# Reordering ScalarE's and VectorE's work in the first groups of a fused retention and feed-forward kernel

## The chip, the cores and the metric

The kernel runs on one core of a Trainium2 chip. The metric is the device time of one execution in microseconds, as the median of several runs. Five engines work beside one another, each on a queue of its own: TensorE (PE, with its weight loads shown apart as PEld), VectorE (DVE), ScalarE (ACT), GpSimd (POOL) and SyncE (SP), which here issues nearly all transfers.

## The reference

Two stages follow one another, in float32 (the weights arrive as 64-bit numbers and are converted on the chip).

```python
# retention: 4 batches, 8 heads, 768 steps, head size 64
for t in range(S):
    state = gamma * state + k[t] (outer) v[t]
    y[t]  = scale * (q[t] @ state)
# x is y with its heads side by side: 3072 tokens by 512
h   = x @ w_in                       # 512 -> 2048
sp  = max(h, 0) + log1p(exp(-|h|))   # softplus
g   = h * erf(sp)
out = g @ w_out                      # 2048 -> 512
```

## The kernel before

**Retention.** The 768 steps of a batch are cut into chunks of 128 tokens, 24 chunks in all. A chunk `j` passes through six steps, written as one-letter names from line 872 on: `K_` scales keys and queries (VectorE, line 403, later 393 and 400), `T` transposes them (TensorE line 418 with ScalarE copies at 424; from chunk 6 on VectorE does it alone, line 413), `S_` forms the scores (TensorE, line 431 or 508), `M` masks them (VectorE, line 443 or 515), `O_` forms the output and the state's increment (TensorE, lines 471, 478 and 487, copied out by ScalarE at 498), and `A` adds the increment to the state (VectorE, line 611).

**Feed-forward, first tile.** The first 512 tokens go through plain products. `hidden(g, u)` forms hidden product `ft = 4 g + u`: four matmuls of 128 x 512, eight records in the trace (line 664), then a copy by ScalarE (line 682). The four products of a group `g` fill one buffer `h`; `gate(g)` runs softplus (line 624) and erf (line 634) over it, each behind a load of its function table; `gated(g)` multiplies h by the result (line 653); `project(g, tt)` multiplies by w_out (line 700). Hidden products use two PSUM banks in turn (`ps_h`), so product `ft` can start only when product `ft - 2` has been copied out. Retention's scores, transposes and outputs share two other banks (`ps_r`).

**Feed-forward, the rest.** From group `G0 = 4` on, 256 tokens at a time go through seven products in place of eight (`hidden_part`, line 757, and `project_part`, line 829). VectorE forms the sums that this needs: of weights at line 248, of x at 740, of the products at 770, 777 and 782.

**Weights.** Each weight piece is loaded raw into parts of the weight buffers that are not in use yet. A conversion takes five VectorE instructions (lines 213, 217, 222, 225, 231) and one ScalarE instruction (line 214), which reads what line 213 wrote and is read by line 225. When line 225 is done the raw piece isn't needed any more, and the next load into its place may be issued. The first four pieces are converted in halves, one product's weights each. `need(...)` drives conversions until the named tile is there; `pace(n)` drives some steps of it between other work. So weight conversion and retention share VectorE's queue, and what is written first in the program stands first in it.

**The order around the change.** A table `after` holds, for each of the first four groups and each of its four products, two lists of calls: those made at once behind the product, and those put on the list `waiting`, which the next paced place empties half-way through its share of weight steps. The loop `for g in range(G0)` reads the table. Behind projection steps of group 3 stand chunk 6's `K_` and `T` and, at the last one, chunk 7's. The loop `for g in range(G0, NG)` does the seven-product groups; `first` marks group 4.

Of the kernel before, what the change touches and what calls it, by code (L numbers as in the profile page):

```python
# [22 lines left out]
FG = 4  # L23
# [22 lines left out]
def kernel(  # L46
# [21 lines left out]
    JPC = TCH // C  # L68
# [67 lines left out]
    def w_out_of(ft):  # L136
        half, s, i = ft // (2 * FG), ft % (2 * FG) // FG, ft % FG
        return w_out_sb[:, s, 2 * half : 2 * half + 2, i, :]
# [115 lines left out]
    def weights():  # L254


        pending = [conversion(n) for n in range(n_p)]
        begun = 0
        for n, steps in enumerate(pending):
            for k, _ in enumerate(steps, start=begun):  # L260
                yield
                if n > 4 and n + 1 < n_p and k == 2:
                    next(pending[n + 1])
                    yield
            begun = int(n > 4)
            if pieces[n] == ("out", 5):
                yield from sums("in", 0)
# [5 lines left out]
    weight_steps = weights()  # L273
# [11 lines left out]
    def need(*what):  # L285
        nonlocal room
        while what not in done:
            if next(weight_steps, done) is done:
                next(last_steps)
            room -= 1  # L290
# [315 lines left out]
    def ret_add(j):  # L606
        if j not in SU:
            return
        new = SU[j]
        if j % NC:  # L610
            nc.vector.tensor_tensor(state, state, new, op=ALU.add)
        else:
            nc.vector.tensor_copy(state, new)
        pace(-0.4)
# [4 lines left out]
    def gate(g):  # L619


        name = "r" if g < 4 and g % 2 else "e"
        E[g] = act.tile([P, N], F32, name=name, bufs=1)
        nc.scalar.activation(E[g], HS[g], AF.Softplus)  # L624

        if g:
            gate_erf(g)
# [10 lines left out]
    def pace_around(n):  # L638


        pace(n / 2)
        run(waiting)
        waiting.clear()
        pace(n / 2)

    def run(steps):
        for f, *args in steps:
            f(*args)

    def gated(g):  # L650
        for a in range(2):
            half = slice(a * N // 2, (a + 1) * N // 2)
            nc.vector.tensor_tensor(E[g][:, half], HS[g][:, half], E[g][:, half], op=ALU.mult)  # L653
        pace(-2.2)
# [4 lines left out]
    def hidden_of(ft, t):  # L659

        if ft not in HP_:
            HP_[ft] = ps_h.tile([P, TCH], F32, name="hp")
        for kk in range(n_k):
            nc.tensor.matmul(  # L664
                HP_[ft][:, t], w_in_of(ft, kk), XC[0][:, kk, t],
                start=(kk == 0), stop=(kk == n_k - 1),
            )

    def hidden(g, u):
        ft = g * FG + u  # L670
        if u == 0:
            HS[g] = act.tile([P, N], F32, name="h")
        need("in", ft)
        if ft == 0:
            hidden_of(1, slice(TCH - C))
        hidden_of(ft, slice(TCH) if ft > 1 else slice(TCH - C, TCH))

        if ft < FG:
            need("in", ft + 2)
        if ft == 0:  # L680
            ret_add(JPC - 1)
        nc.scalar.copy(HS[g][:, u * TCH : (u + 1) * TCH], HP_.pop(ft))  # L682
        done.add(("hidden", ft))
        if ft == FG - 1:
            need("in", FG + 3)
        if g:
            pace_around(3.4 if ft > FG else 0)

    def project(g, tt):
        if g == 0 and tt == 0:  # L690
            O[0] = [ps_o.tile([P, d_model], F32, name=f"o{i}") for i in range(TT)]
        step = tt
        if g:
            of = [(tt, u) for u in range(FG)]
        else:
            of = [(step % 2 * 2 + i // 2, step // 2 * 2 + i % 2) for i in range(4)]
        need("out", g * FG + max(u for _, u in of))
        for tt, u in of:
            ft = g * FG + u
            nc.tensor.matmul(  # L700
                O[0][tt].rearrange("p (d c) -> p d c", d=2),
                E[g][:, u * TCH + tt * P : u * TCH + (tt + 1) * P],
                w_out_of(ft),
                start=(ft == 0),
                stop=(ft == n_ft - 1),
            )
        if step == TT - 1:
            done.add(("project", g))
        pace_around(3.4)
# [10 lines left out]
    G0 = n_ft // FG  # L720
# [5 lines left out]
    def chunk_of(g):  # L726
        return TCH // SCH + (g - G0) // 2
# [74 lines left out]
    def g_sums(g):  # L802

        e = {name: E[g][:, i * TCH : (i + 1) * TCH] for name, i in HQ.items()}

        x = {"11": e["11"], "12": e["21"], "21": e["12"], "22": e["22"]}
        for i in range(4):
            x[f"S{i + 1}"] = HS[g][:, i * TCH : (i + 1) * TCH]
        for to, a, b, plus in (
            ("S1", "21", "22", 1), ("S2", "S1", "11", 0), ("S3", "11", "21", 0), ("S4", "12", "S2", 0),  # L810
        ):
            nc.vector.tensor_tensor(x[to], x[a], x[b], op=ALU.add if plus else ALU.subtract)
        G[g] = x
        pace(-2.4)
# [29 lines left out]
    def put_part(m, step):  # L844
# [27 lines left out]
    K_, T, S_, M, O_, A = (  # L872
        ret_scale, ret_transpose, ret_scores, ret_mask, ret_out, ret_add
    )
# [6 lines left out]
    for j in range(JPC - 2):  # L881
# [3 lines left out]
        if j:  # L885
# [27 lines left out]
    after = [  # L913
        [([], [])] * FG,
        [
            ([(K_, 4), (next, weight_steps), (gate_erf, 0), (load, 5)], []),
            ([], []),
            ([(T, 4)], []),
            ([(S_, 4)], []),
        ],  # L920
        [
            ([(O_, 4)], [(A, 4)]),
            ([(T, 5)], []),
            ([(S_, 5)], [(M, 5)]),
            ([(O_, 5), (load_block_scales,)], [(A, 5)]),
        ],
        [
# [7 lines left out]
    for g in range(G0):  # L935
        for u in range(FG):

            if g and u == (2 if g == 1 else 0):
                waiting.append((gated, g - 1))
            hidden(g, u)  # L940
            run(after[g][u][0])
            if (g, u) == (1, 0):
                room = 0.0
            waiting.extend(after[g][u][1])
        gate(g)
        if g:
            for tt in range(TT):
                project(g - 1, tt)
                if g == 1 and tt < 2:
                    waiting.append((K_, 5) if tt else (M, 4))  # L950
                elif g == G0 - 1 and tt == 0:
                    waiting.extend([(K_, JPC + 2), (T, JPC + 2)])
                elif g == G0 - 1 and tt == 1:
                    load(JPC + 4)
                elif g == G0 - 1 and tt == 3:
                    K_(JPC + 3)
                    T(JPC + 3)

    j = JPC + 2
    put = None
    for g in range(G0, NG):
        first = g == G0
        more = j < NJ
        hidden_part(g, 1)
        hidden_part(g, 2)
        if first:
            gated(g - 1)
        if put is not None:  # L970
            for step in range(3):
                put_part(put, step)
        hidden_part(g, 6)
        if first:
            S_(j)
            M(j)
        for _ in range(2):
            next(last_steps, None)
        if put is not None:
            put_part(put, 3)  # L980
            put = None
        if not first:
            g_sums(g - 1)
        hidden_part(g, 5)
        hidden_part(g, 7)
        for _ in range(2):
            next(last_steps, None)
        if first:
            project(g - 1, 0)
        else:  # L990
            project_part(g - 1, 1)
        hidden_part(g, 4)
        hidden_part(g, 3)


        if more and not first:
            sub_visit(j, g)
        elif more:
            O_(j)
            A(j)  # L1000
            SC[j + 1] = [ret_psum(ps_h) for _ in range(2)]
            sub_scores(j + 1)
            sub_mask(j + 1)
        if g + 1 < NG and (g - G0) % 2:
            x_sums(g + 1)
        if more:
            if j + 2 < NJ:
                K_(j + 2)
                T(j + 2)
            if j + 3 < NJ:  # L1010
                load(j + 3)
            j += 1
        if first:
            gate(g)
            for tt in range(1, TT):
                project(g - 1, tt)
            put_first()
        else:
            for p in (2, 4):
                project_part(g - 1, p)  # L1020
            gate(g)
            for p in (5, 6, 7, 3):
                project_part(g - 1, p)
            if (g - G0) % 2 == 0:
                put = chunk_of(g - 1)
        if g == NG - 1:
            last_gated(g)
        else:
            gated(g)

    g, m = NG - 1, chunk_of(NG - 1)
# [55 lines left out]
```

## Time and profile before

| | before |
|---|---|
| time, median of 3 (lowest, highest) | 686.38 us (686.1, 686.8) |
| span of the profiled run | 684.8 us |
| granted TensorE clock | 1.00 |
| VectorE busy, 40.00 to 50.00 | 9.79 of 10.00 us |
| VectorE busy, 60.00 to 70.00 | 9.86 of 10.00 us |
| VectorE busy, 121.18 to 134.90 | 7.12 of 13.72 us |
| one hidden product of 512 tokens on TensorE | 3.43 us (13.74 for four) |
| softplus or erf over a group, with its table load | 1.28 + 1.91 us |
| one VectorE conversion of a whole piece | about 5 us in five instructions |

The first 165 us hold the plain groups, retention's first chunks and all weight conversions; from there on a period of two groups repeats every 26.8 us to the end. The profile lists, for each instruction, its start, its duration and, in square brackets, how long its engine sat idle before it and what ended that. A matmul's end is modelled, so a distance between starts tells more than a busy time.

### The profile page before, as it was taken

What the parts mean: (1) busy time and instruction counts of PE and PEld (TensorE: products, weight loads), DVE (VectorE), ACT (ScalarE), POOL (GpSimd) and SP (SyncE); (2) the same over time, 40 slices, a digit from 0 to 9 for tenths busy, and PEclk for the clock granted to TensorE, in tenths of its full rate; (3) what the DMA queues carried; (4) which work ended last, traced back from release to release, by engine and by line L of the source; (5) the groups of instructions that cost most, each with busy time, mean ns of one, the idle gap of its engine ahead of it and who ended that gap; (6) DMA issues with size and microseconds to landing.
All of it is one profiled execution on the core that took longest, in us unless ns stands there. A gap on an engine that the chain in (4) does not pass through costs nothing.

```text
span 684.8 us, 14442 instructions
## 1 busy us (share of the span) xinstructions
PE 677.2 (99%) x6214; PEld 578.5 (84%) x6214; DVE 389.5 (57%) x609; ACT 255.9 (37%) x291; POOL 5.8 (1%) x21
## 2 busy tenths in 40 slices
PE   9999999999999999999999999999999999999998
PEld 8744544586999999999999999999999999999996
DVE  4899999475944744543663564455544554343224
ACT  3368362415334244144143242341441432423431
POOL 2000000100000000000000000000000000000000
PEclk9999999999999999999999999999999999999999
DMA  9999843333322322221222222222312200000000
GB/s 189 212 226 237 215 136 94 63 62 61 106 36 43 75 41 37 75 44 34 67 46 43 64 45 45 69 40 44 73 34 47 50 28 1 2 32 1 1 32 32
DMA packets 156528, 47.65 MB, mean 70 GB/s; under 512 B 143024, under 2 KB 147376, under 8 KB 156464
## 3 DMA queue, kind: packets, MB, share of 16 engines
q1 hardware_dynamic: 153952, 46.19, 31.4%
q8 instruction: 49, 0.80, 0.5%
q10 hardware_dynamic: 2512, 0.53, 0.5%
q14 instruction: 15, 0.12, 0.1%
HBM read 40.39 MB, written 6.29 MB: 68 GB/s over the span
## 4 chain that ended last, share of the span: by engine, by line
PE 90%; DVE 7%; issue 1%; DMA 1%; ACT 1%; SPq 0%; POOL 0%; DVEq 0%; POOLq 0%
PE hp L757 37%; PE o L829 36%; PE o L700 6%; PE hp L664 3%; PE r L543 1%; PE hp L508 1%; PE o L377 1%; PE o L579 1%; DMA w_out_sb<-in_moe_w_out_dram 1%; DVE w_out_sb L222 1%; DVE w_out_sb L217 1%; PE r L431 1%; DVE w_in_sb L225 1%; DVE w_out_sb L225 1%; DVE w_out_sb L231 1%
## 5 line engine op out<-in xcount | busy, mean ns | idle before, releaser
L757 PE MATMUL hp<-xs,w_in_sb 128*128 128x128 f32 x1280 | 149.7, 275 | 0.0
L757 PEld LDWEIGHTS hp<-xs,w_in_sb 128*128 128x128 f32 x1280 | 147.8, 192 | 1.6 <-issue 0.5
L829 PE MATMUL o<-w_out_sb,h 128*128 128x256 f32 x640 | 141.7, 379 | 0.0
L829 PEld LDWEIGHTS o<-w_out_sb,h 128*128 128x128 f32 x640 | 121.6, 190 | 16.5
L757 PE MATMUL hp<-xT,w_in_sb 128*128 128x128 f32 x960 | 113.7, 275 | 0.0
L757 PEld LDWEIGHTS hp<-xT,w_in_sb 128*128 128x128 f32 x960 | 111.9, 192 | 1.9 <-issue 1.0
L829 PE MATMUL o<-w_out_sb,e 128*128 128x256 f32 x480 | 112.1, 383 | 0.0
L653 DVE TENSOR_TENSOR e<-h,e 128x1024 f32<-128x1024 f32 x42 | 49.6, 1222 | 101.8 <-ACT e L634 101.8
L829 PEld LDWEIGHTS o<-w_out_sb,e 128*128 128x128 f32 x480 | 88.2, 190 | 11.6
L664 PE MATMUL hp<-xT,w_in_sb 128*128 128x512 f32 (+2 forms) x144 | 57.2, 550 | 1.2 <-ACT h L682 1.2
L782 DVE TENSOR_TENSOR h<-h,hp 128x512 f32<-128x512 f32 x20 | 13.8, 688 | 75.1 <-PE hp L757 75.1
L624 ACT ACT_TABLE_LOAD x24 | 30.8, 1283 | 60.8 <-issue 45.4
L664 PEld LDWEIGHTS hp<-xT,w_in_sb 128*128 128x128 f32 x144 | 25.6, 190 | 28.5 <-issue 23.9
L634 ACT ACTIVATE e<-e 128x2048 f32<-128x2048 f32 (+1 forms) x23 | 42.1, 1836 | 0.2
L624 ACT ACTIVATE e<-h 128x2048 f32<-128x2048 f32 x22 | 42.0, 1910 | 0.2
L775 ACT COPY h<-hp 128x512 f32<-128x512 f32 x20 | 11.7, 587 | 61.0 <-PE hp L757 61.0
L780 ACT COPY h<-hp 128x512 f32<-128x512 f32 x20 | 11.7, 586 | 60.2 <-PE hp L757 60.2
L770 DVE TENSOR_TENSOR h<-h,hp 128x512 f32<-128x512 f32 x20 | 13.7, 686 | 35.7 <-PE hp L757 35.7
L773 ACT COPY h<-hp 128x512 f32<-128x512 f32 x20 | 11.7, 587 | 57.1 <-PE hp L757 57.1
L634 ACT ACT_TABLE_LOAD x24 | 30.8, 1283 | 0.4
L597 ACT COPY xT<-r 128x256 f32<-128x256 f32 x32 | 10.4, 375 | 54.8 <-PE r L543 54.8
L768 ACT COPY h<-hp 128x512 f32<-128x512 f32 x20 | 11.8, 588 | 48.6 <-PE hp L757 48.6
(136 smaller groups left out, 673.7 us busy)
## 6 DMA issues: line engine op xcount, KB each, us to landing
w_out_sb<-in_moe_w_out_dram SPq DMA_DIRECT2D x14, 512.0 KB, 5.9
kq<-in_k_dram SPq DMA_DIRECT2D x23, 256.0 KB, 4.4
v<-in_v_dram SPq DMA_DIRECT2D x23, 256.0 KB, 3.1
out_dram<-r SPq DMA_DIRECT2D x23, 256.0 KB, 3.2
kq<-in_q_dram SPq DMA_DIRECT2D x288, 16.0 KB, 1.8
kb<-in_k_dram SPq DMA_DIRECT2D x288, 16.0 KB, 1.7
w_in_sb<-in_moe_w_in_dram SPq DMA_DIRECT2D x8, 512.0 KB, 12.2
w_out_sb<-in_moe_w_in_dram SPq DMA_DIRECT2D x8, 256.0 KB, 8.7
```

The costliest lines, as they stand in the source:

```text
L225: nc.vector.scalar_tensor_tensor(power, hi, 1 << 31, power, op0=ALU.bitwise_and, op1=ALU.bitwise_or)
L624: nc.scalar.activation(E[g], HS[g], AF.Softplus)
L634: nc.scalar.activation(E[g][:, half], E[g][:, half], AF.Erf)
L653: nc.vector.tensor_tensor(E[g][:, half], HS[g][:, half], E[g][:, half], op=ALU.mult)
L664: nc.tensor.matmul(HP_[ft][:, t], w_in_of(ft, kk), XC[0][:, kk, t], start=(kk == 0), stop=(kk == n_k - 1),)
L700: nc.tensor.matmul(O[0][tt].rearrange("p (d c) -> p d c", d=2), E[g][:, u * TCH + tt * P : u * TCH + (tt + 1) * P], w_out_of(ft), start=(f ...
L757: nc.tensor.matmul(bank[:, u, :], w_in_sb[:, s, IN[a], kk, u * P : (u + 1) * P], XS[m][b][:, kk, :], start=(p in (1, 2, 5) and u == 0 and ...
L768: nc.scalar.copy(h["11"], flat)
L770: nc.vector.tensor_tensor(h["11"], h["11"], flat, op=ALU.add)
L773: nc.scalar.copy(h["12"], flat)
L782: nc.vector.tensor_tensor(h["12"], h["12"], flat, op=ALU.add)
L829: nc.tensor.matmul(O[m][i][:, half, :], G[g][a][:, u * P : (u + 1) * P], w_out_sb[:, s, OUT[b], u, :], start=i not in started, stop=(s == ...
```

## The change

Four places move; the instructions stay the same.

- At the end of group 0 only the weights of hidden product 6 are asked for, no longer those of product 7. These are asked for behind product 4 (`need("in", FG + 3)`), after chunk 4's `K_`, in place of one step of conversion.
- Group 0's erf (`gate_erf(0)`) is written behind product 5, no longer behind product 4.
- Chunk 4's `A` and chunk 5's `M` are called at once and no longer put on the waiting list.
- Chunk 7's `K_` and `T` leave the last projection step of group 2 (in the loop's round `g = 3`) for the first seven-product group, behind its seventh product.

It is for ScalarE to copy hidden products out before it starts on longer work, for VectorE to do retention's steps before weight steps, and for VectorE not to hold a wait for chunk 7's load in front of work that others need.

```diff
         if ft == FG - 1:
-            need("in", FG + 3)
+            need("in", FG + 2)
...
         [
-            ([(K_, 4), (next, weight_steps), (gate_erf, 0), (load, 5)], []),
-            ([], []),
+            ([(K_, 4), (need, "in", FG + 3), (load, 5)], []),
+            ([(gate_erf, 0)], []),
             ([(T, 4)], []),
             ([(S_, 4)], []),
         ],
         [
-            ([(O_, 4)], [(A, 4)]),
+            ([(O_, 4), (A, 4)], []),
             ([(T, 5)], []),
-            ([(S_, 5)], [(M, 5)]),
+            ([(S_, 5), (M, 5)], []),
             ([(O_, 5), (load_block_scales,)], [(A, 5)]),
         ],
...
                 elif g == G0 - 1 and tt == 1:
                     load(JPC + 4)
-                elif g == G0 - 1 and tt == 3:
-                    K_(JPC + 3)
-                    T(JPC + 3)
...
         if first:
+            K_(j + 1)
+            T(j + 1)
             project(g - 1, 0)
```

## The prediction

> **What bounds the kernel now.** I read the page's busy line first, then the list of waits on TensorE, then the timelines of TensorE, ScalarE and VectorE around each wait.
>
> ```profile
> PE 677.2 (99%) x6214; PEld 578.5 (84%) x6214; DVE 389.5 (57%) x609; ACT 255.9 (37%) x291; POOL 5.8 (1%) x21
> ```
>
> TensorE (PE) has work nearly all the time, so another engine's edit pays only where TensorE waits for that engine. The waits name two such places:
>
> ```profile
> PE hp L664 <- ACT h L682: 1.2, 2, 1.1
> PE r L471 <- DVE am L443: 0.4, 2, 0.3
> ```
>
> These sums are too small, because a matmul's modelled end reaches into the gap behind it. I measure from starts. TensorE:
>
> ```profile
> 49.32 3.70 PE L664 MATMUL hp<-xT,w_in_sb 128*128 128x512 f32 x8 [1.05 <-ACT h L682]
> 52.86 1.04 PE L418 MATMUL r<-ident,kq 128*128 128x128 f32 x8
> 54.06 3.70 PE L664 MATMUL hp<-xT,w_in_sb 128*128 128x512 f32 x8 [0.17 <-ACT h L682]
> 57.69 1.16 PE L431 MATMUL r<-qT,kT 64*128 64x128 f32 x16
> ...
> 87.27 3.70 PE L664 MATMUL hp<-xT,w_in_sb 128*128 128x512 f32 x8
> 91.23 0.43 PE L471 MATMUL r<-qT,state 64*64 64x128 f32 x2 [0.27 <-DVE am L443]
> 91.83 0.66 PE L471 MATMUL r<-qT,state 64*64 64x128 f32 x14 [0.17 <-DVE am L443]
> 92.42 1.09 PE L478 MATMUL r<-am,v 128*64 128x128 f32 x16
> ```
>
> Undisturbed distances, from elsewhere in the same timeline: a hidden product to the next one 3.43 us (four in 13.74, from 107.28), a hidden product to a retention step 3.53 (72.62 to 76.15), chunk 5's transposes 0.88 (81.77 to 82.65), its scores 1.09 (86.18 to 87.27), L471 0.60 (76.15 to 76.75). Product 5's last weight load is at 47.25; at 0.429 a step product 6 could start at 48.11. So the losses are: product 6, 49.32 - 48.11 = 1.21; product 7, 54.06 - (52.86 + 0.88) = 0.32; chunk 4's scores, 57.69 - (54.06 + 3.53) = 0.10; chunk 5's output, 92.42 - (87.27 + 3.53 + 0.60) = 1.02. **Sum 2.65 us.** From 93.44 on I find no wait: the step lengths repeat to 0.1, and the later periods are 26.8 each.
>
> ScalarE causes the first two:
>
> ```profile
> 44.84 0.72 ACT L214 ACTIVATE w_in_sb<-w_in_sb,below 128x512 uint32<-128x512 uint32 x1 [2.01 <-DVE w_in_sb L213]
> 45.59 1.28 ACT L624 ACT_TABLE_LOAD   x1
> 46.88 1.91 ACT L624 ACTIVATE e<-h 128x2048 f32<-128x2048 f32 x1
> 48.70 0.57 ACT L682 COPY h<-hp 128x512 f32<-128x512 f32 x1
> 49.16 1.15 ACT L214 ACTIVATE w_out_sb<-w_out_sb,below 128x1024 uint32<-128x1024 uint32 x1
> 50.33 1.28 ACT L634 ACT_TABLE_LOAD   x1
> 51.62 1.91 ACT L634 ACTIVATE e<-e 128x2048 f32<-128x2048 f32 x1
> 53.44 1.06 ACT L682 COPY h<-hp 128x512 f32<-128x512 f32 x2
> ```
>
> The softplus waits behind a weight step that waits 2.01 for VectorE; the copy of product 4 (its matmuls end near 44.8) waits behind the softplus, and product 6 needs its bank. Product 5's copy waits behind the erf, and product 7 needs that bank. VectorE (DVE) causes the fourth:
>
> ```profile
> 87.50 0.69 DVE L213 TENSOR_SCALAR w_in_sb<-w_in_sb 128x1024 uint32<-128x1024 uint32 x1
> 88.10 1.22 DVE L225 SCALAR_TENSOR_TENSOR w_out_sb<-w_in_sb,w_out_sb 128x1024 uint32<-128x1024 uint32 x1
> 89.35 1.23 DVE L231 SCALAR_TENSOR_TENSOR w_in_sb<-w_out_sb 128x1024 f32<-128x1024 f32 x1
> 90.50 1.28 DVE L443 TENSOR_TENSOR am<-r,causal 128x512 f32<-128x512 f32 x2
> ```
>
> Chunk 5's scores are ready at 87.3, but its mask stands behind three weight instructions, and L471 needs the banks that the mask frees. VectorE is full here (13.29 of 13.50 busy from 80.00), so its order decides.
>
> **The Trainium skill.** "Perfetto Trace Analysis", Optimization Strategy: find the gaps on the contended engine and what each waits for; done above. "PSUM — Partial Sum Buffer", Engine vs sequencer instructions: ScalarE's and VectorE's queues are strict FIFO. The trace agrees: the copy at 48.70 had its data near 44.8. "ScalarE: Activation LUTs", What ACT_TABLE_LOAD costs: 1283 ns a load plus a drain of 1380. The load agrees (1.28), but no separate drain shows: 45.59 to 48.70 is 3.11 for load and function. I use 3.11.
>
> **The change, part by part.** No instruction is added or removed; queues are reordered.
>
> 1. *w_in tile 7's conversion leaves the end of group 0.* The softplus now follows tile 6's L214 (42.11, 0.75 to the next): 42.86, plus 3.11, so the copy of product 4 starts at 45.97, 2.14 ahead of when product 6 wants the bank. Gain 1.21.
>
> 2. *Chunk 4's scale (1.14) goes ahead of that conversion.* Its load landed about 42.1 (issued 32.69, 9.4 to landing), VectorE arrives at 44.39: no wait; even counted from the issue's end it lands at 44.84. Tile 7's L213 comes at 45.53, its L225 at 46.97. Added wait: L225 needs tile 7's L214, now queued behind softplus and copy: 46.43 + 0.72, so L225 at 47.17. Bound 0 to 0.20; I take 0.20, and all of VectorE's queue moves by about 0.22. Tile 7 is ready at 48.5; product 7 wants it at 52.5.
>
> 3. *The erf goes behind product 5's copy.* That copy runs at 48.30 and product 7's bank is free by 48.9. Transposes then run 51.64 to 52.52, product 7 at 52.52: gain 0.32. The erf still follows the L214 of 49.2 and ends at 53.59, as now (53.53). Behind it are product 6's copy and chunk 4's two transpose copies, ending near 55.0; scores want them at 56.05, and the 0.10 goes too. The gating product moves ahead of one L213 and so waits for the erf until 53.62; VectorE is then 0.48 behind before. Its gating ends at 55.9, projection 0 wants it at 57.15.
>
> 4. *Masks and state adds at once.* Chunk 5's mask passes the three weight instructions: it starts at 87.50 + 0.48 = 87.98, frees its banks at about 88.66 and 89.26. TensorE, 1.63 ahead, arrives at 87.27 - 1.63 + 3.53 = 89.17. Only the second bank is late, by 0.1. Gain 1.02 - 0.11 = 0.91. What the mask overtakes (w_in and w_out tiles ending by 92) is not wanted before 104. Chunk 4's mask delays a w_in tile to about 67.7; product 8 wants it at 70.98.
>
> 5. *Chunk 7's five instructions move.* Now they stand at 127.72 to 139.6, of which 8.81 is a wait for the kb load, paced by SyncE's issues of 0.43 to 0.5 and landing at about 137.2. Behind them sit the add L770 and chunk 6's mask. This hides today: L770 ends 140.26, its bank is rewritten at 141.29. With TensorE 2.5 earlier, that bank is wanted at 138.8, and about 1.5 would come back. Moved, they start near 146.2, when the load has long landed, take 3.1 and end near 149.4; chunk 7's scores want them at 153.56 - 2.54 = 151.0. Behind them is the add L782, whose product ends only about then. Direct gain 0; it protects 1.5.
>
> Sum: 1.21 + 0.32 + 0.10 + 0.91 = **2.54 us; 686.38 - 2.54 = 683.84**. The tail is pure TensorE order, so the lead is kept to the end.
>
> **Rivals.**
> (a) *VectorE gives part back.* Tile 7's L225 also frees a staging buffer, so SyncE's next loads leave up to 1.3 later (46.53 to 47.84). The tightest lands at 68.43, for an L213 at 70.06: with 1.3 added 69.8 against 70.5, still in time, but the DMA is full there (share 1.0). If it comes 0.8 too late, the mask does too: 683.84 + 0.8 = 684.6. For: full DMA. Against: 12 to 15 us from issue to landing means a deep queue that a late issue doesn't empty.
> (b) *No gain.* VectorE is over 98% busy from 40 to 121; were it the true bound, the lead would be waited for later: 686.4. Against: after 93.44 TensorE shows no wait on it, and VectorE idles 8.81 at 128.
> (c) *Slower.* Chunk 7's work slips behind L782 (product 3 ends near 149.6): 150.3 plus 3.1 is 153.4, and scores wait 2.4. With a front gain of only 1.3, 686.38 - 1.3 + 2.4 = 687.5. For: 1.6 of slack is not much. Against: L782 stands behind it in program order.
>
> **How the numbers follow.** Forecast 0.69, (a) 0.18, (b) 0.08, (c) 0.05. The bound for faster is 685.0. Forecast and most of (a) lie below it: faster 0.84; the rest of (a) and nearly all of (b): same 0.10; slower 0.06. Range: the low end is all 2.65 less 0.4 for the spread of runs, 683.3; the high end takes in (a), 684.9.
>
> **What would show it.** Right: products 6 and 7 start at about 48.1 and 52.5 without a wait on L682; projection 0 at 57.15; chunk 5's L471 near 89.2, with at most 0.1 to 0.3 behind the mask; L700 of group 1 near 90.9; L400 of kb without its 8.8 wait; no new wait between 130 and 180. Wrong: a DMA wait at an L213 or L403 between 60 and 72, L471 still 0.5 or more behind L443, or L508 near 151 waiting for L413.

## The result, and the profile after

| | before | after |
|---|---|---|
| time, median of 4 runs each | 686.59 us (686.1 to 687.36) | 683.82 us (683.54 to 683.93) |
| ratio, 95% interval | | 0.9958 [0.9941, 0.9975] |
| span of the profiled run | 684.8 us | 682.2 us |

The change makes the kernel 2.8 us faster by the medians; the ratio puts it at 0.42%, with 0.25 to 0.59 as its interval. The profiled spans differ by 2.6. The forecast was 683.84.

The busy line of the kernel after, and its list of waits on TensorE (waiting tile, what it waited for; us in total, times, longest):

```profile
PE 676.2 (99%) x6214; PEld 578.5 (85%) x6214; DVE 389.5 (57%) x609; ACT 256.1 (38%) x291; POOL 5.8 (1%) x21
```

```profile
PE o L377 <- POOL ident masks.py:199: 1.5, 1, 1.5
PE r L431 <- ACT qT L424: 0.8, 1, 0.8
PE r L478 <- DVE am L443: 0.2, 1, 0.2
PE hp L478 <- DVE am L443: 0.2, 1, 0.2
```

The busy line has hardly moved. The two waits that the prediction named (hidden products on ScalarE's L682, chunk 5's output on VectorE's L443) are gone. The other four stood in the list of before with the same figures. TensorE's timeline after (start, duration, instruction, tile, count):

```profile
29.84 21.85 PE L664 MATMUL hp<-xT,w_in_sb 128*128 128x384 f32 x64
51.52 1.04 PE L418 MATMUL r<-ident,kq 128*128 128x128 f32 x8
52.40 3.60 PE L664 MATMUL hp<-xT,w_in_sb 128*128 128x512 f32 x8
55.93 1.16 PE L431 MATMUL r<-qT,kT 64*128 64x128 f32 x16
57.02 14.00 PE L700 MATMUL o<-w_out_sb,e 128*128 128x512 f32 x32
...
85.50 3.70 PE L664 MATMUL hp<-xT,w_in_sb 128*128 128x512 f32 x8
89.13 0.75 PE L471 MATMUL r<-qT,state 64*64 64x128 f32 x16
89.81 1.09 PE L478 MATMUL r<-am,v 128*64 128x128 f32 x16
90.84 14.00 PE L700 MATMUL o<-w_out_sb,r 128*128 128x512 f32 x32
```

Product 6 no longer begins a row of its own. It is the last part of one unbroken row from 29.84 to chunk 4's transposes at 51.52. In the kernel before, a row began at 29.85 as well, so the starts can be compared directly:

```profile
29.85 18.41 PE L664 MATMUL hp<-xT,w_in_sb 128*128 128x384 f32 x56
```

TensorE's lead over before is 52.86 - 51.52 = 1.34 us at the transposes, 1.66 at product 7, 1.76 at chunk 4's scores, 1.77 at the product of 85.50, 2.61 at L478 and 2.60 at group 1's projection. It stays there: chunk 7's scores (L508) start at 150.95, where before had 153.56.

ScalarE after, in the stretch that the prediction showed of before:

```profile
42.84 1.28 ACT L624 ACT_TABLE_LOAD   x1
44.13 1.91 ACT L624 ACTIVATE e<-h 128x2048 f32<-128x2048 f32 x1
45.95 0.57 ACT L682 COPY h<-hp 128x512 f32<-128x512 f32 x1
46.41 0.72 ACT L214 ACTIVATE w_in_sb<-w_in_sb,below 128x512 uint32<-128x512 uint32 x1
48.29 0.59 ACT L682 COPY h<-hp 128x512 f32<-128x512 f32 x1 [1.15 <-PE hp L664]
49.22 1.15 ACT L214 ACTIVATE w_out_sb<-w_out_sb,below 128x1024 uint32<-128x1024 uint32 x1 [0.35 <-DVE w_out_sb L213]
50.39 1.28 ACT L634 ACT_TABLE_LOAD   x1
51.68 1.91 ACT L634 ACTIVATE e<-e 128x2048 f32<-128x2048 f32 x1
```

The copy of product 4 starts at 45.95 (45.97 was worked out), not at 48.70. Ahead of the copy at 48.29 the idle time is now ended by TensorE: ScalarE waits for the product instead of holding it up. VectorE after:

```profile
87.89 1.28 DVE L443 TENSOR_TENSOR am<-r,causal 128x512 f32<-128x512 f32 x2
89.09 0.68 DVE L213 TENSOR_SCALAR w_in_sb<-w_in_sb 128x1024 uint32<-128x1024 uint32 x1
89.69 1.22 DVE L225 SCALAR_TENSOR_TENSOR w_out_sb<-w_in_sb,w_out_sb 128x1024 uint32<-128x1024 uint32 x1
...
135.98 0.69 DVE L770 TENSOR_TENSOR h<-h,hp 128x512 f32<-128x512 f32 x1 [7.81 <-PE hp L757]
...
146.66 0.68 DVE L400 TENSOR_TENSOR kb<-kb,kq_b 128x512 f32<-128x512 f32 x1
...
149.57 0.69 DVE L782 TENSOR_TENSOR h<-h,hp 128x512 f32<-128x512 f32 x1 [0.41 <-PE hp L757]
```

Chunk 5's mask stands ahead of the weight steps. VectorE's idle time of 7.81 before L770 is ended by TensorE; in the kernel before, it stood in front of L400 and was ended by a DMA:

```profile
137.18 0.69 DVE L400 TENSOR_TENSOR kb<-kb,kq_b 128x512 f32<-128x512 f32 x1 [8.81 <-DMA kb<-in_k_dram]
```

Chunk 7's work now lies between 146 and 149.2, before L782 had its data.

SyncE's queue (SPq: loads being issued) shows the price, first before, then after:

```profile
89.34 0.88 SPq L174 DMA_DIRECT2D w_in_sb<-in_moe_w_out_dram  x2
...
128.08 7.54 SPq L95 DMA_DIRECT2D kb<-in_k_dram  x16
```

```profile
90.93 1.39 SPq L174 DMA_DIRECT2D w_in_sb<-in_moe_w_out_dram  x2
...
129.67 8.61 SPq L95 DMA_DIRECT2D kb<-in_k_dram  x16
```

The weight load L174 may go once the weight step L225 has read the old piece. L225 stands behind the mask now and ends at 90.91, and the load goes at 90.93. Everything behind it on SyncE is later too: chunk 7's last key load is issued at 129.67 + 8.61 = 138.28, before at 135.62. Of these 2.7 us, 1.6 are there when the first of its 16 key loads is issued; the rest is the last issue alone, which takes 1.49 us where each of the others takes 0.43. Why it does isn't shown.

### The profile page after: what moved, and what is told of

It is laid out like the page before. It is cut to its first block, busy times and chain, and to the rows that moved or that the text cites. A ratio compares the mean times of both kernels' runs of the same rounds, so it can differ in the third digit from the quotient of the medians.

```text
span 682.2 us, 14444 instructions
## 1 busy us (share of the span) xinstructions
PE 676.2 (99%) x6214; PEld 578.5 (85%) x6214; DVE 389.5 (57%) x609; ACT 256.1 (38%) x291; POOL 5.8 (1%) x21
## 4 chain that ended last, share of the span: by engine, by line
PE 98%; ACT 0%; issue 0%; DVE 0%; POOL 0%; POOLq 0%
PE hp L757 37%; PE o L829 36%; PE hp L664 8%; PE o L700 8%; PE r L543 1%; PE hp L508 1%; PE r L431 1%; PE o L377 1%; PE o L579 1%; PE r L478 1%; PE hp L558 1%; PE r L558 1%; PE r L418 0%; PE r L487 0%; PE r L471 0%
## 5 line engine op out<-in xcount | busy, mean ns | idle before, releaser
L757 PE MATMUL hp<-xs,w_in_sb 128*128 128x128 f32 x1280 | 149.7, 275 | 0.0
L757 PEld LDWEIGHTS hp<-xs,w_in_sb 128*128 128x128 f32 x1280 | 147.8, 192 | 1.6 <-issue 0.5
L757 PE MATMUL hp<-xT,w_in_sb 128*128 128x128 f32 x960 | 113.7, 275 | 0.0
L757 PEld LDWEIGHTS hp<-xT,w_in_sb 128*128 128x128 f32 x960 | 111.9, 192 | 1.9 <-issue 1.0
L782 DVE TENSOR_TENSOR h<-h,hp 128x512 f32<-128x512 f32 x20 | 13.8, 688 | 72.3 <-PE hp L757 72.3
L770 DVE TENSOR_TENSOR h<-h,hp 128x512 f32<-128x512 f32 x20 | 13.8, 688 | 42.0 <-PE hp L757 42.0
```

The lines of the kernel that those rows point to most:

```text
L757: nc.tensor.matmul(bank[:, u, :], w_in_sb[:, s, IN[a], kk, u * P : (u + 1) * P], XS[m][b][:, kk, :], start=(p in (1, 2, 5) and u == 0 and ...
L770: nc.vector.tensor_tensor(h["11"], h["11"], flat, op=ALU.add)
L782: nc.vector.tensor_tensor(h["12"], h["12"], flat, op=ALU.add)
```

## The experiments

Distances between starts on TensorE separate three stretches; they don't depend on when the first products begin, which differs by up to 0.8 us between kernels whose opening is the same. *Front* is from the long row of hidden products (29.84 after) to group 1's projection (90.84); *middle* from there to chunk 7's first scores L508; *behind* from L508 to the next L757 row. Each stretch is of one profiled run, in us; the time is the median of that kernel's runs, with its ratio to the kernel before on the same chip (median 686.30 for e1 to e4, 686.26 for the others). The ratio counts all runs, so where some are long it lies above what the two medians give: five of e1's 21 runs took 688.9 to 690.5.

| kernel | front | middle | behind | time | ratio, 95% |
|---|---|---|---|---|---|
| before | 63.59 | 60.12 | 11.02 | 686.59 | |
| after | 61.00 | 60.11 | 11.03 | 683.82 | 0.9958 [0.9941, 0.9975] |
| e1 front alone | 62.66 | 62.95 | 11.03 | 687.07 | 1.0019 [1.0010, 1.0028] |
| e2 masks alone | 62.68 | 62.06 | 11.03 | 686.89 | 1.0014 [1.0005, 1.0024] |
| e3 chunk 7 alone | 63.57 | 60.11 | 11.03 | 686.57 | 1.0004 [0.9995, 1.0012] |
| e4 all but chunk 7 | 61.04 | 67.30 | 11.03 | 690.76 | 1.0063 [1.0051, 1.0076] |
| e5 all but masks | 62.62 | 60.12 | 11.02 | 685.25 | 0.9984 [0.9978, 0.9991] |
| e6 erf not moved | 61.68 | 60.11 | 11.03 | 684.43 | 0.9974 [0.9964, 0.9984] |
| e7 chunk 7 late | 60.99 | 62.58 | 12.73 | 687.38 | 1.0012 [1.0004, 1.0021] |
| e8 load before mask | 62.33 | 60.11 | 11.03 | 685.11 | 0.9984 [0.9977, 0.9992] |
| e9 load after mask | 61.01 | 60.11 | 11.03 | 683.54 | 0.9960 [0.9946, 0.9973] |

**e1, the front alone.** Of the change, only group 0's end and the first list:

```diff
-            need("in", FG + 3)
+            need("in", FG + 2)
...
-            ([(K_, 4), (next, weight_steps), (gate_erf, 0), (load, 5)], []),
-            ([], []),
+            ([(K_, 4), (need, "in", FG + 3), (load, 5)], []),
+            ([(gate_erf, 0)], []),
```

> Only the edits to the first two groups' weights and erf; masks, state adds and chunk 7 as before. Theory 1 (VectorE's place for chunk 5's mask sets the end of the stretch): TensorE gains 1.63 us up to product 8 and waits it back at chunk 5's output. The changed pacing puts the mask one weight instruction earlier than before, at about 89.85, so the second bank is free at about 91.15 in place of 91.8; net gain 0.65, less about 0.1 at chunk 7's load: 685.8 us. Theory 2 (each edit brings its own share): gain 1.63, less what chunk 7's load takes back, 684.8 to 685.3 us.

It was slower, against both. The front gained 0.93, and the middle lost 2.83. The wait is in VectorE's timeline:

```profile
139.69 0.69 DVE L400 TENSOR_TENSOR kb<-kb,kq_b 128x512 f32<-128x512 f32 x1 [10.37 <-DMA v<-in_v_dram]
```

Before, this L400 started at 137.18. Here chunk 7's load comes 2.5 later, its work still stands in front of L770, and L757 waits 2.8 for L770's bank. SyncE's last issue for the keys ends 1.35 later (136.97). What holds it up is not the mask but a weight step further on: VectorE's L225 at 100.21 waits 1.02 for ScalarE, and the load L174 behind it goes at 101.47 in place of 100.39. The other 1.2 us of the delay aren't explained by the issues. The profiled run took 688.08, 1.0 more than the median, so the median run loses about 1.7 in the middle.

**e2, the masks alone.**

```diff
-            ([(O_, 4)], [(A, 4)]),
+            ([(O_, 4), (A, 4)], []),
...
-            ([(S_, 5)], [(M, 5)]),
+            ([(S_, 5), (M, 5)], []),
```

> Only chunk 4's state add and chunk 5's mask called at once; the rest as before. Theory 1: products 6 and 7 start at 49.3 and 54.1 as before, chunk 5's output no longer waits (1.02 us gained), but the weight step behind the mask is later, so SyncE issues chunk 7's loads later; kb lands between 137.6 and 138.7 in place of 137.2, the add behind it ends 0.4 to 1.5 us too late for its bank, and the time is 685.8 to 686.9 us. Theory 2: gain 1.02, so 685.4 us, with no wait at the seven-product group.

Also slower, as theory 1 had it. The front gained 0.91, against the 1.02 at which the prediction put the mask's cost; why they differ stands in point 4 below. But the middle lost 1.94 by the same wait on L770: L400 started at 139.11.

**e3, chunk 7's move alone.** The last two hunks of the diff, nothing else.

> Only chunk 7's scale and transposes moved into the first seven-product group. Both theories: nothing on TensorE's path waited for them before, so the time is that of before, 686.4 us within 0.3; the wait of 8.8 us at the kb load is gone from VectorE's row. A rival, that VectorE's idle time itself cost something, would give less than 685.5 us.

No change, as expected: none of the three stretches moves. VectorE's wait of 8.8 us at L400 was idle time that cost nothing.

**e4, all but chunk 7's move.** The kernel after, with chunk 7's two steps left where before had them:

```diff
                     load(JPC + 4)
+                elif g == G0 - 1 and tt == 3:
+                    K_(JPC + 3)
+                    T(JPC + 3)
...
         if first:
-            K_(j + 1)
-            T(j + 1)
             project(g - 1, 0)
```

> All edits but chunk 7's. In the trace of the changed kernel SyncE's last kb issue for chunk 7 ends at 138.3 and would land near 140.0, not at the 137.2 of before. Theory A (the load itself got later, because SyncE's loads wait for weight steps that now stand behind the mask): the add on the h11 quarter ends at about 143.1, its bank is wanted at 138.7, TensorE waits 4.4 us, 688.2 us, slower than before. Theory B (as in the prediction, load at 137.2): 1.5 us come back, 685.3 us.

Its front is that of after, 61.04, and the middle gives back 7.2. The wait on TensorE, VectorE's L400, TensorE's rows and the clock (in the last, by stretches: length, PE, PEld, DVE, ACT, POOL busy, then the granted clock, DMA share, GB/s):

```profile
PE hp L757 <- DVE h L770: 4.4, 1, 4.4
```

```profile
139.63 0.69 DVE L400 TENSOR_TENSOR kb<-kb,kq_b 128x512 f32<-128x512 f32 x1 [11.21 <-DMA kb<-in_k_dram]
```

```profile
142.77 6.58 PE L757 MATMUL hp<-xs,w_in_sb 128*128 128x128 f32 x32 [4.38 <-DVE h L770]
```

```profile
138.00:142.00 4.00, 0.39 (x8) 0.20 (x4) 2.37 (x4) 0.00 (x0) 0.00 (x0) 0.97 0.66 142
142.00:146.00 4.00, 3.23 (x15) 3.23 (x16) 4.00 (x6) 0.00 (x0) 0.00 (x0) 0.50 0.24 37
146.00:150.00 4.00, 4.00 (x21) 3.58 (x21) 2.54 (x3) 0.58 (x1) 0.00 (x0) 0.68 0.23 36
150.00:154.00 4.00, 4.00 (x20) 2.51 (x19) 2.96 (x3) 0.00 (x0) 0.00 (x0) 1.00 0.21 33
```

SyncE's last key issue ends at 138.24 and the keys are used from 139.63. TensorE wanted the bank at 138.32: the row ahead began at 135.35, and without a wait the next one follows 2.97 later, as from 138.32 to this line of the kernel before:

```profile
141.29 3.84 PE L757 MATMUL hp<-xs,w_in_sb 128*128 128x128 f32 x32
```

In e4 that next row started at 142.77: 4.45 lost. After that pause the clock is at half, and that row takes 6.42 to the next start in place of 3.68: 2.74 more. "TensorE: Matmul & The Clock Gate", What's actually happening, says that the clock gate passes half of the pulses after an idle window of about 3.4 us, and all again after about as long a busy one. This trace agrees with it: 0.50 after a pause of 4.4; a shorter pause, in e7, doesn't fit so simply. Theory A had the wait of 4.4 right and 688.2 us for it; the loss by the clock came on top. So without chunk 7's move the change would be a loss of 4.5 us.

**e5, all but the masks.** The kernel after, with `A` of chunk 4 and `M` of chunk 5 on the waiting list as before (the reverse of e2's diff).

> The whole change except that chunk 4's state add and chunk 5's mask stay on the waiting list. Theory 1 (the mask's place decides, and chunk 7's move only keeps what was gained): as in the run of the first edits alone, TensorE waits about 0.5 us for the late state add and about 1.3 us for chunk 5's mask, but nothing is lost at the seven-product group: 683.8 + 1.7 = 685.5 us. Theory 2 (each edit its share): 683.8 + 0.9 = 684.7 us.

Faster than before, 1.43 slower than after. The whole of that is in the front (62.62 against 61.00), where TensorE stands behind the mask (VectorE's line first):

```profile
89.40 1.28 DVE L443 TENSOR_TENSOR am<-r,causal 128x512 f32<-128x512 f32 x2
```

```profile
90.13 0.43 PE L471 MATMUL r<-qT,state 64*64 64x128 f32 x2 [0.37 <-DVE am L443]
90.73 0.66 PE L471 MATMUL r<-qT,state 64*64 64x128 f32 x14 [0.17 <-DVE am L443]
```

The front's edits alone bring only 0.97 of their 1.77, because the mask doesn't come forward with TensorE: counted from the start of the long row it is 1.63 later than in after, and the front is 1.62 longer. Of this, 0.67 goes already at chunk 5's transposes, the second half of which waits for chunk 4's late state add (L611); what that add's place is worth by itself was not tested.

**e6, the erf not moved.**

```diff
-            ([(K_, 4), (need, "in", FG + 3), (load, 5)], []),
-            ([(gate_erf, 0)], []),
+            ([(K_, 4), (need, "in", FG + 3), (gate_erf, 0), (load, 5)], []),
+            ([], []),
```

> The whole change except that the erf of group 0 stays behind product 4. As the prediction has it (the erf's place makes product 7 wait), product 7 waits 0.3 us: 684.1 us, mask unaffected. Rival: product 5's copy starts at about 50.3, before product 7 wants the bank at 52.4, so that wait doesn't come back; but the weight step on ScalarE now stands behind the erf, VectorE waits for it by 0.9 us near 51, everything on its queue moves, and chunk 5's mask frees its second bank 0.65 us late: 684.4 to 684.5 us, the loss at chunk 5's output and not at product 7.

The time is 0.6 above after. By the prediction's reading the loss would be at product 7, but there is none: it starts 0.88 behind the transposes (51.10 to 51.98), although the copy of product 5 is 1.55 later than in after. The loss sits nearly 40 us further on. ScalarE and VectorE first, then the mask, then TensorE:

```profile
49.84 0.57 ACT L682 COPY h<-hp 128x512 f32<-128x512 f32 x1
```

```profile
51.49 1.23 DVE L225 SCALAR_TENSOR_TENSOR w_out_sb<-w_out_sb 128x1024 uint32<-128x1024 uint32 x1 [0.86 <-ACT w_out_sb L214]
```

```profile
88.15 1.28 DVE L443 TENSOR_TENSOR am<-r,causal 128x512 f32<-128x512 f32 x2
```

```profile
88.89 0.43 PE L471 MATMUL r<-qT,state 64*64 64x128 f32 x2
89.48 0.66 PE L471 MATMUL r<-qT,state 64*64 64x128 f32 x14 [0.17 <-DVE am L443]
```

The erf in front puts ScalarE's L214 later, and VectorE waits 0.86 for it. In after, VectorE's only wait between 50 us and the mask is one of 0.18, for the erf; e6 has no other than this one. So the mask is 0.68 later, counted from the start of the long row (58.73 against 58.05), and TensorE pays just that there: front 61.68 against 61.00.

**e7, chunk 7 late.** Its `K_` and `T` one place further back:

```diff
         if first:
-            K_(j + 1)
-            T(j + 1)
             project(g - 1, 0)
...
         hidden_part(g, 3)
+        if first:
+            K_(j + 1)
+            T(j + 1)
```

> The whole change, but chunk 7's scale and transposes stand behind the last of the seven products and its add, not behind the seventh. Theory 1 (1.5 to 1.8 us of slack where the change puts them): they start at about 150.3, end at 153.3, chunk 7's scores are wanted at 150.95 and wait 2.4 us: 686.2 us. Rival (slack is larger than read): below 685 us.

Rival (c) is real in this place. TensorE, then its clock:

```profile
152.98 0.69 PE L508 MATMUL hp<-qT,kT 64*64 64x64 f32 x32 [2.40 <-DVE qT L413]
153.60 12.26 PE L700 MATMUL o<-w_out_sb,r 128*128 128x512 f32 x24
```

```profile
152.00:156.00 4.00, 3.02 (x36) 1.75 (x37) 2.50 (x6) 3.96 (x4) 0.00 (x0) 0.81 0.18 29
156.00:160.00 4.00, 4.00 (x8) 1.62 (x7) 1.95 (x4) 1.72 (x1) 0.00 (x0) 0.76 0.72 147
```

The wait is the 2.4 that the prediction worked out. In this run a stretch at half clock follows, worth 1.70 in the column *behind*: in steps of half a microsecond the granted clock is 1.00 until 154.5, 0.50 to 157.5 and 1.00 again from 158.0, some 3.4 us at half. The runs tell it too: five of the 13 took 686.0 to 686.4 at a mean clock of 1.00 (the 2.4 alone), eight took 687.3 to 688.2 at 0.997 or 0.998.

**e8 and e9, the same load before and behind the mask.** Two products of a scratch tile with itself on VectorE, added to the kernel after; GpSimd fills the tile at the start, and nothing else reads it:

```diff
...
+    def ballast():
+        for _ in range(2):
+            nc.vector.tensor_tensor(ballast_t, ballast_t, ballast_t, op=ALU.mult)
...
-            ([(S_, 5), (M, 5)], []),
+            ([(S_, 5), (ballast,), (M, 5)], []),     # e8
+            ([(S_, 5), (M, 5), (ballast,)], []),     # e9
```

> The changed kernel with two needless VectorE instructions on a scratch tile (about 1.25 us together) directly ahead of chunk 5's mask. Theory 1 (VectorE bounds TensorE up to that mask, with no slack left): the mask's second bank comes 1.2 us later and the time is 685.0 us. Rival (VectorE has slack there): 683.8 us.

> The changed kernel with the same two needless VectorE instructions (about 1.3 us), now directly behind chunk 5's mask in place of ahead of it. Theory 1 (behind that mask no work of TensorE waits for VectorE before the seven-product groups, and chunk 7's block has 1.5 us of slack against the load): 683.8 us, within 0.3. Rival (VectorE bounds the whole stretch up to 121 us): as with the load ahead of the mask, 685.0 us.

VectorE of e8 with TensorE behind it, then VectorE of e9:

```profile
87.80 1.41 DVE L877 TENSOR_TENSOR ballast<-ballast 128x512 f32<-128x512 f32 x2
```

```profile
89.86 0.43 PE L471 MATMUL r<-qT,state 64*64 64x128 f32 x2 [0.75 <-DVE am L443]
```

```profile
88.24 1.28 DVE L443 TENSOR_TENSOR am<-r,causal 128x512 f32<-128x512 f32 x2
89.44 1.41 DVE L877 TENSOR_TENSOR ballast<-ballast 128x512 f32<-128x512 f32 x2
```

1.3 us of VectorE's time in front of the mask cost 1.29 (front 62.33 against 61.00); the same behind it cost nothing. So up to this mask VectorE sets the time; from there on it has at least these 1.3 us of slack, although it is as full (7.86 of the 8.00 us from 88.00 busy in both after and e9).

**e10 and e12, further.** e10 brings chunk 3's scale and transpose forward as well; e12 adds to e10 that chunk 5's mask goes ahead of one more weight step:

```diff
     S_(JPC - 2)
+    K_(JPC - 1)
     A(JPC - 3)
+    T(JPC - 1)
     M(JPC - 2)
     ret_out(JPC - 2, copies=False)
-    K_(JPC - 1)
...
-    T(JPC - 1)
...
-            ([(S_, 5), (M, 5)], []),                              # e12
+            ([(pace, -1), (S_, 5), (M, 5), (pace, 1)], []),       # e12
```

> The changed kernel with chunk 3's scale and transposes ahead of chunk 2's mask and output, so that chunk 2's output fills the time of the transposes' copies (TensorE waits 0.8 us for them at 23 us, and 0.3 for a mask). Theory 1: TensorE gains about 0.8 us up to product 8, VectorE only about 0.4, so chunk 5's mask, which has no slack, gives back 0.3 to 0.4: 683.3 to 683.5 us. Rival (gains add up): 683.0 us.

> As the run with chunk 3 early, and chunk 5's mask one weight instruction (1.15 us) further forward. Theory 1: the mask then has about 0.7 us of slack and the whole 0.8 us stays: 683.0 us. Rival (the gain at 23 us is lost on the way to product 1, whose weights VectorE converts then): 683.8 us.

e10 took 683.22 us (682.85 to 683.49), ratio 0.9954 [0.9942, 0.9967]; e12 took 683.62 (682.99 to 684.03), 0.9959 [0.9947, 0.9972]. Their long row of hidden products began at 29.02 and 28.98, in the eleven other kernels between 29.41 and 30.18, so the wait at the start is gone as meant. e12's front is 60.92, and its L471 runs 0.60 without a wait; the 0.1 that after still loses there is gone too. Neither is told apart from after by its time, so a version that beats it wasn't shown.

## Why the prediction was right, point by point

1. *Tile 7 leaves group 0's end, 1.21.* The lead at chunk 4's transposes is 1.34. The mechanism was right; the size was 0.13 short. The traces account for 0.11 of it: where product 6 starts afresh, as in the kernel before, its first weight load starts together with it (both at 49.32) and the transposes follow 3.54 later; inside a row each weight load starts one step ahead, and a product takes 3.43. The prediction compared the start of a row with one inside a row. No run tells this step apart from the next one.

2. *Chunk 4's scale ahead, L225 at 47.17.* It started at 47.17 with a wait of 0.18 for L214 (0.20 taken).

3. *The erf behind product 5's copy, 0.32 and 0.10.* Sizes right: the lead grows by 0.32 at product 7 and 0.10 at the scores. The attribution was wrong: e6 shows that step 1 alone takes product 7's wait away. With step 1, the softplus is done earlier, and the copy of product 5 is early enough even behind the erf. What the erf's place brings is 0.6 through step 4, by keeping VectorE from waiting. The prediction saw no such link from ScalarE's order to the mask. Softplus and erf with their table load again took 3.11 (42.84 to 45.95 and 50.39 to 53.50).

4. *Chunk 5's mask, 0.91.* The mask started at 87.89 (87.98 worked out), the lead grew by 2.60 - 1.77 = 0.83. TensorE lost 0.08 between L471 and L478 for the second bank, where 0.11 was foreseen. The rest is a mis-sized distance: the prediction put L471 3.53 behind the product, but it comes at 3.63 in after, in e2 and in e12 alike, also where L471 then runs its undisturbed 0.60 (e2, e12). So the late mask had cost 0.92 and not 1.02, and e2's front got back just that. The marks it had set were met: product 6 at 48.09 (51.52 less 3.43), product 7 at 52.40, projection 0 at 57.02, L471 at 89.13, group 1's projection at 90.84.

5. *Chunk 7's move, 0, protecting 1.5.* Direct gain 0 was right (e3). The term protected was mis-sized: 6.9, the distance from e4 to after. The prediction took the load's landing from the kernel before, about 137.2, and looked only at TensorE being earlier. In fact the same edits make the load later (139.63 in e4): SyncE's loads wait for a weight step that the mask has overtaken, and without the masks' edits for another one (e1, and e5, where L174 goes at 101.67). The long pause then halves the clock. That error didn't touch the time because the whole change includes the move. The slack of about 1.6 us in its new place was right: after ends this work at 149.16 and starts L508 at 150.95, and e7's next place fails by 2.4.

The sum was 2.54 for a measured 2.77 (2.6 by the spans), with +0.13 in step 1 and -0.08 in step 4. That 683.84 met 683.82 so closely is luck: the two errors nearly cancel, and the 686.38 from which it was counted became 686.59 with a fourth run. That the parts came out so close hides that they don't add: alone they give +0.8, +0.6 and +0.3 (the last not told from 0), together -2.8.

*Rivals.* (a) didn't happen as told: between 60 and 72 no VectorE step waits for a DMA. The mechanism it named, late issues on SyncE, was real 60 us later and only hidden by step 5. One such wait is new in after: L400 of chunk 8 at 157.70 waits 4.54 for its keys, and costs nothing: TensorE's rows behind it keep their lead of 2.6 (L757 at 161.98 and 165.55, before at 164.58 and 168.16). So the prediction's sign "no new wait between 130 and 180" was met for TensorE, not for VectorE. (b) is out behind the mask, by e9 and by the middle column; up to the mask VectorE does set the time (e8). (c) exists one place further on (e7). That its 687.5 lies near e7's 687.38 is chance: it took a front gain of 1.3 and no loss of clock.

## What to carry to other kernels

When an engine's order decides, price an edit with the whole set it belongs to: an earlier consumer is worth only as much as the next producer comes forward with it (e5), and a weight step put off holds back the load that reuses its buffer, and every load queued behind that one (e4). A wait that is hidden today needs its slack recomputed with both ends moved, the wanter earlier and the load later. Put the same small load before and behind a suspect instruction (e8, e9): the pair tells in two runs up to where an engine sets the time.

## What the runs showed of the hardware that was not expected

- A pause of TensorE costs more than its length when the clock drops: 2.74 us beyond 4.45 in e4, 1.70 beyond 2.4 in e7's profiled run, where the drop came 1.5 us after TensorE was back at work (152.98, half clock from 154.5). The length alone doesn't tell. The page cited under e4 speaks of an idle window of about 3.4 us, and 2.4 is shorter; by their times and mean clocks eight of e7's 13 runs had the drop, while e1's profiled run kept 1.00 after 2.8 and five of its 21 runs had it. That the place of the pause in a free-running window decides, as that page describes the window, would fit only if a window need not be idle throughout; this was not tested. A few runs without such a pause show the lower mean clock too (two of e3's 13, 0.998, and one of e8's 16, 0.997), so not every drop need come from the pause named here.
- SyncE's issues set when the keys are there. The 16 key loads of chunk 7 take 7.54 us in the kernel before, 0.43 for each and 0.47 from one start to the next, and half of them land within 1.7 us of their issue. So chunk 7's keys are as late as these issues begin, and later still by any issue that is long, such as the last one of after (1.49) and of e4 (1.32).
